# Attention and two feed-forward stages on one core: the operands of the next token tile, the places of the buffers, the leaky function, and full rows in the attention

## The chip, the cores and the metric

One Trainium2 chip, one core. The metric is the device time of one launch in microseconds (us), the median of several runs. TensorE (PE) multiplies, VectorE (DVE), ScalarE (ACT) and GpSimd (POOL) work on elements, SyncE (SP) issues the transfers. SBUF is the working memory, PSUM the eight banks that PE writes.

## What is computed

Three stages, all in float32, each on the result of the one before:

- attention: 4 batches, 8 heads, 576 positions, head size 64; causal, with a decay bias from a running sum of max(s, 0): `softmax(q k^T / 8 + min(bias, 0)) v`
- experts: 2304 tokens of width 512, 8 experts of width 1024; every token goes through every expert: `out += P[:, e] * (max(x @ w1[e], 0) @ w2[e])`, where P comes from 8 rounds of normalising the gate over rows and columns
- last stage: `h = x @ w_in` (width 2048), `g = max(0.01 h, h)`, `out = g @ w_out`

## The kernel before

**Units.** Experts and last stage run over three tiles of 2 x 384 tokens (j = 0, 1, 2). A unit is one tile against 256 columns of the first weight and the 256 rows of the second that go with them: 32 units for each tile in the experts (n = 0 to 95), 8 in the last stage (96 to 119). A tile change is at n = 32, 64, 96, 104 and 112.

**First product.** It is done in seven products of half size (P1 to P7, Strassen's scheme in Winograd's form), on sums and differences of quarters of the token tile (the operands, x = 0 to 6) and of the weight (made in `weights1`). Every operand is held as a high part and a low part (what the high part lacks), and a product is six matmuls of 384 columns: high x high, high x low, low x high, for two halves of the width (`product`, L809 to L811).

**Operands of a tile** (`operands`). Four differences on DVE (L161), for which there are two places, XT[0] and XT[1], each used twice: `b12 - b11`, `b22 - XT[0]`, `b22 - b12`, `b21 - XT[1]`. Seven casts on ACT to the high parts XO (L154), and seven subtractions to the low parts (L156), five on DVE and two on POOL. XO exists once. So the third difference waits for the cast and subtraction of the first, and each operand of the new tile waits until the last product of the old one that reads it is done. All have key n - 0.5 and wait for `("begun", n - 1)`, the first product of the unit before.

**After the products** (`first`). PE adds products up in four banks a, b, c, d; DVE adds what is common (L818). `out` then makes a block of the hidden layer, 384 columns in a high part hh and a low part hl (tile HB). Experts: ACT takes max(., 0) from the bank to hh (L830), DVE subtracts hh from the bank (L831). Last stage, four steps: ACT copies the bank to G (L835), DVE takes max(0.01 x bank, G) to G (L836), ACT casts G to hh (L837), DVE subtracts hh from G (L838).

**Second product** (`second`). Six chunks a unit, c0 to c5, six matmuls of 512 columns each (L877 to L879), in three Y banks in turn, which DVE adds to acc (L896 experts, L902 last stage). They run one unit late, between the products: P1, P6, c0, P5, c1, P7, c2, P2, c3, P4, c4, P3, c5.

**Other work of DVE.** The weights of the last stage come in 64-bit form and are made to float32 in 32 conversions of eight steps (L780 to L787), one in every odd unit from 9 to 71. At the end of each expert tile PE turns the 24 blocks of acc into X (L914).

**Order.** Nothing is scheduled by the chip: `Plan.order` plays all tasks through with estimated times, gives each engine the ready task with the lowest key, and the program is written out in that order. Each engine then works strictly in it. A unit n has keys n to n + 1.

**Attention.** 16 pairs of heads. Per pair: loads (`load_raw`), transposes of q and k in five blocks, the fifth with the 64 rows that are left (`t_pe`, L367), scores (L416 to L422), maximum and exponential, transposes of the result (L469, L471), and the product with v in `pv0` and `pv1`, the last part again with 64 rows (L497).

Of the kernel before, what the change touches and what calls it, by code (L numbers as in the profile page):

```python
# [102 lines left out]
def fused_kernel(ctx: ExitStack, tc: tile.TileContext, q, k, v, s, w_gate, w1, w2, w_in, w_out, out):  # L103
# [18 lines left out]
    wg = const.tile([128, 4, 32], F32, name="wg")  # L122
    P = const.tile([128, NTT, E], F32, name="P")

# [22 lines left out]

    def operands(do, j, key, rd=None):
        t0, t1 = slice(W * j, W * j + W), slice(HALF + W * j, HALF + W * j + W)
        b11, b12, b21, b22 = X[:, 0:2, t0], X[:, 0:2, t1], X[:, 2:4, t0], X[:, 2:4, t1]  # L150
        rd = rd or [("X", j)]

        def split(i, src, res, lo_eng):
            do("act", key + 0.001 * i, pa(768), lambda: nc.scalar.copy(XO[:, i, 0], src), res, [("xh", i)])  # L154
            do(lo_eng, key + 0.001 * i, pd(768) if lo_eng == "dve" else pgg(768),
               lambda: (nc.vector if lo_eng == "dve" else nc.gpsimd).tensor_tensor(out=XO[:, i, 1], in0=src, in1=XO.bitcast(F32)[:, i, 0], op=ALU.subtract),  # L156
               res + [("xh", i)], [("xl", i)])

        def comb(eng, i, dst, x, y, res, out):
            do(eng, key + 0.001 * i - 0.002, pd(768) if eng == "dve" else pgg(768),  # L160
               lambda: (nc.vector if eng == "dve" else nc.gpsimd).tensor_tensor(out=dst, in0=x, in1=y, op=ALU.subtract), res, [out])  # L161

        comb("dve", 0, XT[0], b12, b11, rd, "xt0")
        comb("dve", 0, XT[1], b22, XT[0], rd + ["xt0"], "xt1")
        split(0, b11, rd, "dve")
        split(1, XT[1], ["xt1"], "dve")
        split(2, XT[0], ["xt0"], "pool")
        comb("dve", 3, XT[0], b22, b12, rd, "xt0")
        split(3, XT[0], ["xt0"], "dve")
        split(4, b21, rd, "pool")  # L170
        comb("dve", 5, XT[1], b21, XT[1], rd + ["xt1"], "xt1")
        split(5, XT[1], ["xt1"], "dve")
        split(6, b22, rd, "dve")
# [55 lines left out]
    with ExitStack() as actx:  # L229
# [24 lines left out]
        PC = [ac.tile([128, 4, 2, 320], F32, name=f"PC{i}") for i in range(PB)]  # L254
        PD = [ac.tile([64, 2, 64], F32, name=f"PD{i}") for i in range(PB)]
        EB = ac.tile([128, NE, 512], F32, name="EB")
# [104 lines left out]
        def t_pe(p, which, raw, first=False):  # L361
# [3 lines left out]
            for t in range(5):  # L365
                w = 128 if t < 4 else TAIL
                nc.tensor.transpose(tp[0:n, 128 * t:128 * t + w], raw[0:w, t, 0:n // 64, :].rearrange("p h d -> p (h d)"), ident[0:w, 0:w])  # L367

# [104 lines left out]
        def p_copy(n, part, eng):  # L473
# [3 lines left out]
            if part == 1:  # L477
                dst, src = PD[p % PB], t[0:TAIL, 0, :].rearrange("p (h q) -> p h q", h=2)
            elif i == 8:
# [24 lines left out]
        def pv1(p, part):  # L504
# [38 lines left out]
        for p in range(2):  # L543
            add(("L", "v", p), "sp", -5 + 4 * p, 950, lambda p=p: load_raw(RV[p], v, p), [("qd", 0, 1), ("kd", 0, 1)], DMA)
        add(("c0",), "dve", -40, 370, relu_s, [("s",)])
# [267 lines left out]
    def first(n):  # L813
# [11 lines left out]
        def out(block, bank, key):  # L825
# [3 lines left out]
            if kind == "moe":  # L829
# [3 lines left out]
                return  # L833
            g = G[block]
# [87 lines left out]
    for n, (kind, j, u) in enumerate(seq):  # L922
# [42 lines left out]
```

## Time and profile before

| | |
|---|---|
| runs, us | 2203.02, 2204.18, 2206.31; median 2204.18 |
| profiled execution | 2205.11 us, span on the core 2203.3 us |
| busy share | PE 97%, DVE 75%, POOL 64%, ACT 41% |
| mean granted clock of PE | 0.988 |
| attention | about 0 to 230 us |
| experts, units 0 to 95 | about 230 to 1790 us |
| last stage, units 96 to 119 | about 1790 to 2203 us |

Starts of the sixth product (bank b, L809 FB), which mark a unit: 731.4 (n = 31), 751.2 (32), 777.9 (33), 794.1 (34), 1251.8 (63), 1773.1 (95), 1905.5 (103), 2040.5 (111). Away from tile changes they lie 15.76 us apart.

In the rows below, `[2.55 <-DVE HB L831]` means that the engine stood idle for 2.55 us before this instruction, and that DVE's work of line 831 on tile HB released it. In groups, `xN | busy, mean` is the number of instructions, their us in all and the mean in ns.

### The profile page before, as it was taken

Reading aid. Unit: us, or ns where it says so; the run is one execution under the profiler, and the core shown is the slowest. Engines: PE = TensorE matmul, PEld = TensorE weight load, DVE = VectorE, ACT = ScalarE, POOL = GpSimd, SP = SyncE. Lnnn points to the kernel's source line nnn. Section 1 sums busy time; section 2 is a strip of 40 time slices with the busy share of each in tenths; the row PEclk is TensorE's granted clock in tenths of the full one; section 3 lists DMA queues with packets and bytes.
Section 4 is the critical chain, followed back from the end, with each engine's and each line's share of the span. In section 5 each row is a group of like instructions: output and inputs, shape, how many; then the busy total and the mean of one; then the engine's idle time right before and its main releaser. Section 6 shows DMA issues by size and latency. Waiting matters only on the chain.

```text
span 2203.3 us, 30513 instructions
## 1 busy us (share of the span) xinstructions
PE 2139.7 (97%) x10919; PEld 1879.8 (85%) x10919; DVE 1661.7 (75%) x2800; ACT 900.1 (41%) x1746; POOL 1406.5 (64%) x1207
## 2 busy tenths in 40 slices
PE   7998999999999899999999989999999999999899
PEld 6776689999999798999999878899999988889798
DVE  5888486887788878788778878765656577978877
ACT  5887423232323342333333343333333344444542
POOL 6777656666666666666666656656565676766662
PEclk9999999999999999999999989999999999999999
DMA  6553212222332222232323222222222222122221
GB/s 146 133 135 84 87 58 68 96 87 90 96 96 82 76 87 90 96 96 81 97 96 96 72 86 72 81 65 68 67 68 66 69 65 64 51 97 66 86 68 48
DMA packets 177057, 183.78 MB, mean 83 GB/s; under 512 B 69866, under 2 KB 131306, under 8 KB 176906
## 3 DMA queue, kind: packets, MB, share of 16 engines
q1 hardware_dynamic: 176906, 181.84, 27.7%
q8 instruction: 86, 1.41, 0.3%
q14 instruction: 65, 0.53, 0.1%
HBM read 158.67 MB, written 13.42 MB: 78 GB/s over the span
## 4 chain that ended last, share of the span: by engine, by line
PE 87%; DVE 9%; issue 2%; ACT 1%; POOL 1%; SPq 0%; DMA 0%; POOLq 0%; ACTq 0%; DVEq 0%
PE Y L877 14%; PE Y L879 14%; PE Y L878 14%; PE FC L809 4%; PE FD L809 4%; PE FA L809 4%; PE FC L810 4%; PE FD L811 4%; PE FC L811 4%; PE FD L810 4%; PE FA L811 4%; PE FA L810 4%; PE FB L811 2%; PE FB L809 2%; PE FB L810 2%
## 5 line engine op out<-in xcount | busy, mean ns | idle before, releaser
L189 POOL TENSOR_TENSOR WQ<-RB,WQ 128x512 fp32r<-128x512 f32 x360 | 558.1, 1556 | 671.7 <-ACT WQ L209 357.3
L877 PE MATMUL Y<-WQ,HB 128*128 128x512 f32 x1440 | 569.3, 395 | 4.3 <-DVE acc L896 4.3
L879 PE MATMUL Y<-WQ,HB 128*128 128x512 f32 x1440 | 569.0, 395 | 2.5 <-DVE HB L831 2.5
L878 PE MATMUL Y<-WQ,HB 128*128 128x512 f32 x1440 | 566.4, 393 | 0.0
L896 DVE SCALAR_TENSOR_TENSOR acc<-Y,P,acc 128x512 f32<-128x512 f32 x504 | 375.6, 745 | 205.2 <-PE Y L879 205.0
L189 POOL TENSOR_TENSOR RB<-RB 128x256 f32<-128x256 f32 x480 | 375.7, 803 | 10.2 <-DMA RB<-in_moe_w_dram 0.7
L879 PEld LDWEIGHTS Y<-WQ,HB 128*128 128x128 f32 x1440 | 271.5, 189 | 65.4 <-DVE HB L831 2.9
L189 POOL TENSOR_TENSOR WQ<-RAW,WQ 128x1024 fp32r<-128x1024 f32 x120 | 301.1, 2509 | 18.9 <-ACT WQ L226 18.9
L830 ACT ACTIVATE HB<-FB 128x384 fp32r<-128x384 f32 x96 | 47.2, 492 | 633.0 <-DVE FB L818 632.9
L877 PEld LDWEIGHTS Y<-WQ,HB 128*128 128x128 f32 x1440 | 271.8, 189 | 37.7 <-DVE acc L896 5.0
L878 PEld LDWEIGHTS Y<-WQ,HB 128*128 128x128 f32 x1440 | 273.4, 190 | 32.2
L809 PE MATMUL FA<-XO,WQ 128*128 128x384 f32 x480 | 167.4, 349 | 8.1 <-DVE HB L831 6.4
L809 PE MATMUL FD<-XO,WQ 128*128 128x384 f32 x480 | 166.3, 347 | 9.0 <-DVE G L836 7.3
L809 PE MATMUL FC<-XO,WQ 128*128 128x384 f32 x480 | 165.1, 344 | 7.2 <-DVE G L836 5.1
L811 PE MATMUL FA<-XO,WQ 128*128 128x384 f32 x480 | 164.4, 343 | 0.0
L810 PE MATMUL FA<-XO,WQ 128*128 128x384 f32 x480 | 163.6, 341 | 0.0
L811 PE MATMUL FD<-XO,WQ 128*128 128x384 f32 x480 | 163.4, 341 | 0.0
L811 PE MATMUL FC<-XO,WQ 128*128 128x384 f32 x480 | 163.1, 340 | 0.0
L810 PE MATMUL FD<-XO,WQ 128*128 128x384 f32 x480 | 163.0, 340 | 0.0
L810 PE MATMUL FC<-XO,WQ 128*128 128x384 f32 x480 | 162.7, 339 | 0.0
L211 ACT CAST WQ<-RB 128x1024 fp32r<-128x1024 f32 x120 | 125.6, 1046 | 90.2 <-PE FC L810 85.8
L226 ACT CAST WQ<-RAW 128x1024 fp32r<-128x1024 f32 x120 | 126.1, 1051 | 15.9 <-PE Y L879 10.3
(165 smaller groups left out, 3976.5 us busy)
## 6 DMA issues: line engine op xcount, KB each, us to landing
RB<-in_moe_w_dram SPq DMA_DIRECT2D x96, 512.0 KB
RAW<-in_moe_w_dram SPq DMA_DIRECT2D x96, 512.0 KB, 3.7
RB<-win SPq DMA_DIRECT2D x24, 512.0 KB
RAW<-wout SPq DMA_DIRECT2D x24, 512.0 KB, 3.8
bits<-in_moe_w_in_dram SPq DMA_DIRECT2D x16, 512.0 KB, 5.7
bits<-in_moe_w_out_dram SPq DMA_DIRECT2D x16, 512.0 KB
WQ<-WQ SPq DMA_DIRECT2D x48, 144.0 KB, 2.3
RB<-in_k_dram SPq DMA_DIRECT2D x31, 160.0 KB, 2.9
```

The costliest lines, as they stand in the source:

```text
L189: return lambda: nc.gpsimd.tensor_tensor(out=out, in0=x, in1=y, op=op)
L211: do("act", key + 0.04, pa(1024), lambda: nc.scalar.copy(wa[0][:, 0:4], SW), ss, [("wh0", s)])
L226: do("act", key + 0.5, pa(1024), lambda: nc.scalar.copy(wb[0], RAW2), ["raw2"], [("vh", s)])
L809: nc.tensor.matmul(t, lhsT=hi, rhs=xh, start=new, stop=False, skip_group_check=on)
L810: nc.tensor.matmul(t, lhsT=hi, rhs=xl, start=False, stop=False, skip_group_check=on)
L811: nc.tensor.matmul(t, lhsT=lo, rhs=xh, start=False, stop=(k == 1), skip_group_check=on)
L830: do("act", key, pa(W), lambda: nc.scalar.activation(out=hh, in_=src, func=ACTF.Relu), [bank], [("hh", slot)])
L877: nc.tensor.matmul(y, lhsT=hh, rhs=wb[0][:, f], start=(f == 0), stop=False)
L878: nc.tensor.matmul(y, lhsT=hh, rhs=wb[1][:, f], start=False, stop=False)
L879: nc.tensor.matmul(y, lhsT=hl, rhs=wb[0][:, f], start=False, stop=(f == 1))
L896: do("dve", k2, pd(512), lambda a=a, y=y, p=p: nc.vector.scalar_tensor_tensor(out=a, in0=y, scalar=p, in1=a, op0=ALU.mult, op1=ALU.add), [ ...
```

## The change

- The four differences of the next tile have a place each (XT[0], XT[1] and two halves of GG, the former G) and keys n - 2.6 to n - 1.7; they wait for `("begun", n - 3)`. The casts and low parts have keys 0.6 of a unit before the product that reads them. For tile 0 of the experts, made within the attention, all stays but small shifts of keys.
- Conversions leave out units 31, 33, 63 and 65 and go on to unit 79.
- P moves from the first pool to the later one; with two unused tiles (320 and 832 bytes) X, WQ, XO, XT and RB lie 256 bytes lower, RAW2 and G 320 bytes and HB, acc and the tiles after them 1152 bytes higher than before.
- Last stage: ACT applies Prelu in the bank, ACT copies the bank to hh, DVE subtracts hh from the bank.
- Attention: all five transposes take 128 rows; the last part of the product with v takes 128 rows, of which 64 are zeros (set once), so v is loaded in two transfers a head instead of one.

```diff
-    P = const.tile([128, NTT, E], F32, name="P")
+    const.tile([128, 80], F32, name="room")
...
-    def operands(do, j, key, rd=None):
+    def operands(do, j, early, late, rd, room=None):
...
-            do("act", key + 0.001 * i, pa(768), lambda: nc.scalar.copy(XO[:, i, 0], src), res, [("xh", i)])
+            do("act", late[i], pa(768), lambda: nc.scalar.copy(XO[:, i, 0], src), res, [("xh", i)])
...
+        D = XT + (room or XT)
+        names = ["xt0", "xt1"] + (["xt2", "xt3"] if room else ["xt0", "xt1"])
+        parts = [lambda: comb(0, D[0], b12, b11, rd, names[0]),
+                 lambda: comb(1, D[1], b22, D[0], rd + [names[0]], names[1])]
+        more = [lambda: comb(2, D[2], b22, b12, rd, names[2]),
+                lambda: comb(3, D[3], b21, D[1], rd + [names[1]], names[3])]
+        for f in parts + (more if room else []):
+            f()
...
+        def load_v(p):
...
+                nc.sync.dma_start(out=RV[p % 2][:, 0:4, hh, :], in_=flat[r0:r0 + 512].rearrange("(t p) d -> p t d", p=128))
+                nc.sync.dma_start(out=RV[p % 2][0:TAIL, 4, hh, :], in_=flat[r0 + 512:r0 + S])
...
+            for i in range(2):
+                nc.gpsimd.memset(RV[i][TAIL:128, 4, :, :], 0.0)
+                nc.gpsimd.memset(PD[i][TAIL:128, :, :], 0.0)
...
-                nc.tensor.transpose(tp[0:n, 128 * t:128 * t + w], raw[0:w, t, 0:n // 64, :].rearrange("p h d -> p (h d)"), ident[0:w, 0:w])
+                nc.tensor.transpose(tp[0:n, 128 * t:128 * t + 128], raw[:, t, 0:n // 64, :].rearrange("p h d -> p (h d)"), ident)
...
-                                 (768, 64, TAIL, 4, lambda h: d_[:, h, :], False, True)])
+                                 (768, 64, 128, 4, lambda h: d_[:, h, :], False, True)])
...
+    P = wp.tile([128, NTT, E], F32, name="P")
...
-    G = [wp.tile([128, W], F32, name=f"G{i}") for i in range(4)]
+    GG = wp.tile([128, 4, W], F32, name="GG")
+    G = [GG[:, i] for i in range(4)]
+    wp.tile([128, 208], F32, name="room2")
...
-            do("act", key, pa(W), lambda: nc.scalar.copy(g, src), [bank], [("g", block)])
-            do("dve", key, pd(W), lambda: v.scalar_tensor_tensor(out=g, in0=src, scalar=0.01, in1=g, op0=ALU.mult, op1=ALU.max), [bank], [("g", block)])
-            do("act", key + 0.01, pa(W), lambda: nc.scalar.copy(hh, g), [("g", block)], [("hh", slot)])
-            do("dve", key + 0.02, pd(W), lambda: v.tensor_tensor(out=hl, in0=g, in1=hh.bitcast(F32), op=ALU.subtract), [("g", block), ("hh", slot)], [("hl", slot)])
+            do("act", key, pa(W), lambda: nc.scalar.activation(out=src, in_=src, func=ACTF.Prelu, alpha=0.01), [], [bank])
+            do("act", key, pa(W), lambda: nc.scalar.copy(hh, src), [bank], [("hh", slot)])
+            do("dve", key, pd(W), lambda: v.tensor_tensor(out=hl, in0=src, in1=hh.bitcast(F32), op=ALU.subtract), [bank, ("hh", slot)], [("hl", slot)])
...
-            operands(do, j, n - 0.5, [("X", j), ("begun", n - 1)])
+            operands(do, j, [n - 2.6 + 0.3 * i for i in range(4)], [n - 0.6 + at[x] for x in ("P1", "P6", "P5", "P7", "P2", "P4", "P3")],
+                     [("X", j), ("begun", n - 3)], [GG[:, 0:2], GG[:, 2:4]])
...
-        if 9 <= n < 9 + 64 and n % 2:
+        if 9 <= n < 80 and n % 2 and n not in (31, 33, 63, 65):
```

## Rows read from the trace of the kernel before

**Rows 1.** Busy by stretch: five engines (instructions), granted clock, DMA share, GB/s.
```profile
605.30:636.80 31.50, 31.50 (x157) 28.39 (x156) 25.33 (x39) 10.35 (x19) 20.27 (x17) 1.00 0.30 92
699.80:715.60 15.80, 15.80 (x80) 14.25 (x79) 15.70 (x23) 4.79 (x9) 10.54 (x9) 1.00 0.20 58
715.60:731.40 15.80, 15.80 (x80) 14.24 (x80) 9.74 (x17) 5.67 (x11) 9.82 (x9) 1.00 0.39 126
731.40:794.10 62.70, 53.67 (x259) 47.02 (x258) 54.06 (x65) 27.39 (x46) 37.17 (x27) 0.92 0.25 76
1251.80:1315.40 63.60, 56.07 (x260) 48.70 (x260) 54.20 (x65) 27.48 (x46) 37.27 (x27) 0.87 0.23 75
1773.10:1826.70 53.60, 50.49 (x259) 44.57 (x258) 41.96 (x56) 29.65 (x53) 37.78 (x27) 1.00 0.19 59
1858.20:1889.80 31.60, 31.60 (x159) 28.48 (x158) 26.80 (x39) 14.03 (x27) 21.14 (x17) 1.00 0.22 68
1905.50:1946.00 40.50, 33.70 (x158) 29.55 (x158) 37.15 (x49) 18.43 (x34) 24.91 (x18) 0.96 0.19 64
2040.50:2081.80 41.30, 35.29 (x158) 30.88 (x158) 36.94 (x49) 19.82 (x35) 27.51 (x19) 0.92 0.24 77
```

**Rows 2.** Order of time: PE in one pair of the attention, around five transposes.
```profile
88.15 0.27 PE L471 MATMUL tr<-ident,EAB 128*64 128x128 f32 x1
88.26 0.80 PE L367 MATMUL qk<-ident,RB 128*128 128x128 f32 x5
88.99 0.40 PE L421 MATMUL sc<-WQ 128*128 128x288 f32 x1
```

**Rows 3.** Order of time at unit 32: PE instructions that waited (start, us).
```profile
747.00 0.51 PE L877 MATMUL Y<-WQ,HB 128*128 128x512 f32 x1 [2.17 <-DVE acc L896]
...
751.23 0.41 PE L809 MATMUL FB<-XO,WQ 128*128 128x384 f32 x1 [2.55 <-DVE HB L831]
...
756.20 0.69 PE L809 MATMUL FA<-XO,WQ 128*128 128x384 f32 x1 [3.68 <-DVE HB L831]
```

**Rows 4.** Groups by line on DVE from 250 us on, shapes apart.
```profile
L161 DVE TENSOR_TENSOR XT<-X,XT 128x768 f32<-128x768 f32 x10 | 16.4, 1644 | 0.0
L161 DVE TENSOR_TENSOR XT<-X 128x768 f32<-128x768 f32 x10 | 16.3, 1627 | 0.0
L156 DVE TENSOR_TENSOR XO<-X,XO 128x768 fp32r<-128x768 f32 x10 | 20.4, 2040 | 0.0
L156 DVE TENSOR_TENSOR XO<-XT,XO 128x768 fp32r<-128x768 f32 x15 | 20.2, 1356 | 0.0
L836 DVE SCALAR_TENSOR_TENSOR G<-FA,G 128x384 f32<-128x384 f32 x24 | 13.3, 554 | 7.6 <-ACT G L835 7.6
L838 DVE TENSOR_TENSOR HB<-G,HB 128x384 fp32r<-128x384 f32 x96 | 106.1, 1108 | 8.9 <-ACT HB L837 7.3
L831 DVE SCALAR_TENSOR_TENSOR HB<-FA,HB 128x384 fp32r<-128x384 f32 x95 | 52.5, 552 | 21.5 <-ACT HB L830 21.4
```

**Rows 5.** Order of time: starts of P1, P6 and the chunk behind them.
```profile
730.29 0.34 PE L809 MATMUL FA<-XO,WQ 128*128 128x384 f32 x1
...
731.36 0.33 PE L809 MATMUL FB<-XO,WQ 128*128 128x384 f32 x1
...
732.40 0.39 PE L877 MATMUL Y<-WQ,HB 128*128 128x512 f32 x1
```

**Rows 6.** Order of time on ACT: the only load of a table.
```profile
0.73 1.28 ACT L331 ACT_TABLE_LOAD   x1 [0.73 <-PEq L949]
```

**Rows 7.** Chain of work that ended last, one pair of the attention (start, us).
```profile
64.89 1.09 DVE sm L456
...
70.85 0.45 PE sc L416
...
77.04 1.08 DVE sm L456
```

**Rows 8.** Order of time on SP: loads of v for the first pairs.
```profile
16.63 2.23 SPq L296 DMA_DIRECT2D RV<-in_v_dram  x4
```

More of the change, by code (lines that the diff above doesn't have):

```diff
@@ L145, in fused_kernel @@
     pgg = lambda n: 92.0 + n * 2.3
-    def operands(do, j, key, rd=None):
+    def operands(do, j, early, late, rd, room=None):
         t0, t1 = slice(W * j, W * j + W), slice(HALF + W * j, HALF + W * j + W)
         b11, b12, b21, b22 = X[:, 0:2, t0], X[:, 0:2, t1], X[:, 2:4, t0], X[:, 2:4, t1]
-        rd = rd or [("X", j)]
         def split(i, src, res, lo_eng):
-            do("act", key + 0.001 * i, pa(768), lambda: nc.scalar.copy(XO[:, i, 0], src), res, [("xh", i)])
-            do(lo_eng, key + 0.001 * i, pd(768) if lo_eng == "dve" else pgg(768),
+            do("act", late[i], pa(768), lambda: nc.scalar.copy(XO[:, i, 0], src), res, [("xh", i)])
+            do(lo_eng, late[i], pd(768) if lo_eng == "dve" else pgg(768),
@@ L156, in split @@
                lambda: (nc.vector if lo_eng == "dve" else nc.gpsimd).tensor_tensor(out=XO[:, i, 1], in0=src, in1=XO.bitcast(F32)[:, i, 0], op=ALU.subtract),
                res + [("xh", i)], [("xl", i)])
[L159 to L163, printed above, removed]
@@ L164, in operands, with comb @@
-        comb("dve", 0, XT[1], b22, XT[0], rd + ["xt0"], "xt1")
-        split(0, b11, rd, "dve")
[L166 to L169, printed above, removed]
+        def comb(i, dst, x, y, res, out):
+            do("dve", early[i], pd(768), lambda: nc.vector.tensor_tensor(out=dst, in0=x, in1=y, op=ALU.subtract), res, [out])
+        D = XT + (room or XT)
+        names = ["xt0", "xt1"] + (["xt2", "xt3"] if room else ["xt0", "xt1"])
@@ new lines, in operands @@
+        parts = [lambda: comb(0, D[0], b12, b11, rd, names[0]),
[4 more added lines that the diff above has]
+            f()
+        split(0, b11, rd, "dve")
+        split(1, D[1], [names[1]], "dve")
+        split(2, D[0], [names[0]], "pool")
+        if not room:
+            more[0]()
@@ L170, in operands @@
+        split(3, D[2], [names[2]], "dve")
         split(4, b21, rd, "pool")
-        comb("dve", 5, XT[1], b21, XT[1], rd + ["xt1"], "xt1")
-        split(5, XT[1], ["xt1"], "dve")
+        if not room:
+            more[1]()
+        split(5, D[3], [names[3]], "dve")
         split(6, b22, rd, "dve")
@@ L254, in fused_kernel @@
         PC = [ac.tile([128, 4, 2, 320], F32, name=f"PC{i}") for i in range(PB)]
-        PD = [ac.tile([64, 2, 64], F32, name=f"PD{i}") for i in range(PB)]
+        PD = [ac.tile([128, 2, 64], F32, name=f"PD{i}") for i in range(PB)]
         EB = ac.tile([128, NE, 512], F32, name="EB")
@@ L287, in side @@
             return {"a": "act", "d": "dve"}[KEYS["cq" if p % 2 else "cp"][i]]
+        def load_v(p):
+            b, hp = divmod(p, HP)
+            flat = v.rearrange("b h n d -> (b h n) d")
+            for hh in range(2):
+                r0 = (b * H + 2 * hp + hh) * S
+                nc.sync.dma_start(out=RV[p % 2][:, 0:4, hh, :], in_=flat[r0:r0 + 512].rearrange("(t p) d -> p t d", p=128))
+                nc.sync.dma_start(out=RV[p % 2][0:TAIL, 4, hh, :], in_=flat[r0 + 512:r0 + S])
         def load_raw(dst, src, p, heads=(0, 1)):
@@ L365, in t_pe @@
             for t in range(5):
-                w = 128 if t < 4 else TAIL
-                nc.tensor.transpose(tp[0:n, 128 * t:128 * t + w], raw[0:w, t, 0:n // 64, :].rearrange("p h d -> p (h d)"), ident[0:w, 0:w])
+                nc.tensor.transpose(tp[0:n, 128 * t:128 * t + 128], raw[:, t, 0:n // 64, :].rearrange("p h d -> p (h d)"), ident)
         def q_hi(p, h):
@@ L477, in p_copy @@
             if part == 1:
-                dst, src = PD[p % PB], t[0:TAIL, 0, :].rearrange("p (h q) -> p h q", h=2)
+                dst, src = PD[p % PB][0:TAIL], t[0:TAIL, 0, :].rearrange("p (h q) -> p h q", h=2)
             elif i == 8:
@@ L543, in fused_kernel @@
         for p in range(2):
-            add(("L", "v", p), "sp", -5 + 4 * p, 950, lambda p=p: load_raw(RV[p], v, p), [("qd", 0, 1), ("kd", 0, 1)], DMA)
+            add(("L", "v", p), "sp", -5 + 4 * p, 950, lambda p=p: load_v(p), [("setc",), ("qd", 0, 1), ("kd", 0, 1)], DMA)
         add(("c0",), "dve", -40, 370, relu_s, [("s",)])
@@ L566, in fused_kernel @@
                     add(("L", w, p), "sp", b9 - KEY["L"], 950, lambda raw=raw, src=src, p=p: load_raw(raw[p % 2], src, p), [("T", w, p - 2)] + [("L", x, 1) for x in "qkv"], DMA)
-                add(("L", "v", p), "sp", b9 - KEY["L"] + 3, 950, lambda p=p: load_raw(RV[p % 2], v, p), [("pv1", p - 2, 1), ("pv0", p - 2, 0)], DMA)
+                add(("L", "v", p), "sp", b9 - KEY["L"] + 3, 950, lambda p=p: load_v(p), [("pv1", p - 2, 1), ("pv0", p - 2, 0)], DMA)
             if p:
@@ L643, in fused_kernel @@
             plan.writer["X", 0, p] = d["xc", p]
-        operands(plan.do, 0, 9 * NPAIR - 6, [("X", 0, p) for p in (0, 1, 2, 3, 8, 9, 10, 11)])
+        operands(plan.do, 0, [9 * NPAIR - 6 + 0.001 * i for i in (-2, -1, 3, 5)], [9 * NPAIR - 6 + 0.001 * i for i in range(7)],
+                 [("X", 0, p) for p in (0, 1, 2, 3, 8, 9, 10, 11)])
         plan.do("sp", -6, 100, lambda: nc.sync.dma_start(out=wgraw, in_=w_gate.rearrange("(c p) e -> p c e", p=128)), [], ["wgraw"], DMA)
@@ L833, in out @@
                 return
-            g = G[block]
-            do("act", key, pa(W), lambda: nc.scalar.copy(g, src), [bank], [("g", block)])
-            do("dve", key, pd(W), lambda: v.scalar_tensor_tensor(out=g, in0=src, scalar=0.01, in1=g, op0=ALU.mult, op1=ALU.max), [bank], [("g", block)])
-            do("act", key + 0.01, pa(W), lambda: nc.scalar.copy(hh, g), [("g", block)], [("hh", slot)])
-            do("dve", key + 0.02, pd(W), lambda: v.tensor_tensor(out=hl, in0=g, in1=hh.bitcast(F32), op=ALU.subtract), [("g", block), ("hh", slot)], [("hl", slot)])
+            do("act", key, pa(W), lambda: nc.scalar.activation(out=src, in_=src, func=ACTF.Prelu, alpha=0.01), [], [bank])
+            do("act", key, pa(W), lambda: nc.scalar.copy(hh, src), [bank], [("hh", slot)])
+            do("dve", key, pd(W), lambda: v.tensor_tensor(out=hl, in0=src, in1=hh.bitcast(F32), op=ALU.subtract), [bank, ("hh", slot)], [("hl", slot)])
         pe("P1")
```

## Prediction

> **What bounds the kernel now.** I read first the busy time by stretch, then the groups of instructions on VectorE (DVE), then single stretches in order of time. In a plain stretch of the experts TensorE (PE) is busy for all of 31.50 us, which is two units (78 matmuls each), so a unit takes 15.75 us; the same holds in the last stage, 31.60 us for two units and a rest [rows 1]. There nothing but the matmuls counts. The time that can be had lies where a token tile ends and the next begins, five times (units 32, 64, 96, 104, 112). The stretch of units 31 to 33 lasts 62.70 us instead of 47.25; 24 transposes of the finished tile belong in it, at 0.11 us each [rows 2] 2.6 us, so 12.8 us are lost. In the same way 63.60 gives 13.7 and 53.60 gives 3.7 (three units and the transposes each), 40.50 gives 9.0 and 41.30 gives 9.8 (two units) [rows 1]. Together 49 us. PE's waits there end with DVE: 2.17 us for an addition to acc, 2.55 and 3.68 us for the low part of a hidden block [rows 3]. Of that loss a part is the clock: it is granted at 0.92, 0.87, 1.00, 0.96 and 0.92 in the five stretches and at 1.00 beside them [rows 1], and as its other level is half, 0.08 of 62.70 us is 5 us of matmul time given away after the waits. If the waits go, that goes with them.
>
> Why DVE is late: a unit with a conversion takes 15.70 us of DVE in 15.80, one without 9.74, so a conversion is 6.0 us [rows 1]. A tile change adds four differences, two of 1.627 and two of 1.644 us, 6.5 us, and five low parts, two of 2.040 and three of 1.356, 8.1 us [rows 4]. Units 31 and 32 of before thus ask for 9.7 x 2 + 6.0 + 6.5 + 8.1 = 40 us of DVE in 31.5.
>
> **Part 1: differences early, in four places.** They keep their 6.5 us, but may run from unit n-3 on, as they no longer wait for a place that a low part still reads. The conversions of units 31, 33, 63 and 65 go to 73 to 79, where DVE has 6.0 us free in every unit without one [rows 1]. What is left in units n-1 and n: 9.7 x 2 + 8.1 = 27.6 of 31.5 us for units 32, 64 and 96; removed are 12.5 us at the first two and 6.5 at the third, against losses of 12.8, 13.7 and 3.7. Splits now carry keys beside the product that reads them, 0.6 of a unit (9.4 us) ahead. Where the differences land nothing is free at once: units 29 and 30 hold 15.70 + 9.74 + 6.5 = 31.9 us in 31.5. DVE leaves unit 29 up to 3 us behind and is level again in unit 31. Behind a late difference in DVE's queue stand the additions to acc; PE has three Y banks and a chunk every 2.4 us, some 4.8 us of cover. I take 1.5 us of waits left at units 32 and 64 (bounds: nothing, and half the present loss, 6.5) and 0.3 at each of the other three.
>
> **Part 2: leaky function in the bank.** Per block, DVE loses the maximum (0.554 us), and its subtraction reads a bank instead of G: 0.552 us, as the same operation in the experts takes, instead of 1.108 [rows 4]. Four blocks a unit: 4 x (0.554 + 0.556) = 4.4 us off 13.4 (half of 26.80 [rows 1]). ScalarE (ACT) still has two operations of a block each. The bank is held for one more ACT copy, about 0.5 us by the nearest of its kind, and c is wanted again 4.9 us after its last product (a chunk, two products, a chunk; a product is 1.06 us [rows 5], so a chunk (15.75 - 7 x 1.06) / 6 = 1.4), which covers it. At units 104 and 112 DVE has (13.4 - 4.4) x 2 + 8.1 = 26.1 of 31.5 us left to do, where it had 41.4: the 9.0 and 9.8 go but for the 0.3 each. Everywhere else in the last stage PE does not wait, so 4.4 us a unit buys nothing there.
>
> The Trainium skill ("ScalarE: Activation LUTs", section "Table sets: the hidden batching unit") says that cheap functions are in every set, and that a function of another set costs a load. The trace shows one load of 1.28 us for Copy, Relu and Exp together [rows 6]; Prelu is in no row.
>
> Sum of parts 1 and 2: 49 - (2 x 1.5 + 3 x 0.3) = 45 us.
>
> **Part 3: full rows in the attention.** The five transposes of q or k take 0.73 us from 88.26 to 88.99, where five full ones at 0.11 (88.15 to 88.26) would take 0.55 [rows 2]: 0.18 us each, twice a pair, and about as much for the tail of the product with v. That would be 0.54 x 16 = 9 us, were PE the bound all the way. The chain of waits says otherwise: in a pair of 12.15 us (64.89 to 77.04) it is on DVE and ACT up to 70.85 and on PE from there [rows 7]. Only what is saved after 70.85 counts, one group of transposes a pair; the other and the tail of v lie beside the DVE stretch, and PE waits there that much longer. 0.18 x 13 pairs in this rhythm: 2.3 us. Bounds 0 and 9.
>
> The Trainium skill ("TensorE: Matmul & The Clock Gate", section "LDWEIGHTS (loading the stationary operand)") says that columns count and rows don't. By that, 64 more columns in each of 32 groups would cost 0.05 x 32, about 2 us, and save nothing. The row speaks against it: the 64-row step and the one ahead of it are the slow ones.
>
> SP issues four loads of v more before the first pairs, at 2.23 / 4 = 0.56 us each: 2.2 us [rows 8], and the bias of pair 1 is queued behind them. I take 1 us of it on the path (0 to 2.2). Later pairs have two loads more per 12 us; fourteen at 0.56 us are 8 us of SP, and v is wanted a pair later. The four memsets stand on POOL ahead of these loads and are in this term.
>
> **Part 4: places.** All buffers from X on move down by 256 bytes, HB and acc up by 1152; the matmuls stay the same. No row shows a matmul at another place. The nearest: two blocks of the same six matmuls, 1.07 and 1.04 us (730.29, 731.36, 732.40) [rows 5], 178 and 173 ns a matmul, so 5 ns either way on 9360 matmuls, -47 to +47 us as far bounds. I take 0: the slow and the fast block read slices of the same tiles, a whole number of 512 bytes apart, and differ by where they stand in the order.
>
> **Forecast.** 45 + 2.3 - 1 = 46 to 47 us. The profiled execution took 2205.1 us (span 2203.3), 0.04% over the median of 2204.2, which is less than two runs differ. 2204.2 - 47 = 2157 us.
>
> **Rivals.**
> *The wait moves ahead.* Units 29 and 30 are over-full by the sum above, and 61 and 62 as well. If the additions to acc fall behind there, PE waits and the clock falls before the tile change instead of at it. For: 31.9 of 31.5 us. Against: DVE stood at 15.70 of 15.80 in unit 29 without one wait of PE. Units 32 and 64 would then give back half, 13 us, and the ends of the last stage keep 2 each: 2157 + 13 - 3 + 6 = 2173 us.
> *Table loads.* If Prelu's table lacks Copy, each block of the last stage brings two loads: 8 x 1.28 = 10.3 us a unit on top of 7.0 (half of 14.03), 17.3 in 15.75, so 1.5 x 24 = 37 us: 2194 us. For it: no row has Prelu. Against: one load served three functions. The Trainium skill ("ScalarE: Activation LUTs", section "What ACT_TABLE_LOAD costs") gives a switch 2.66 us with its drain, by which this rival would be estimated at 8 x 2.66 + 7.0 - 15.75 = 12.5 us a unit, 300 us in all.
> *Places cost.* If the moved addresses put every matmul 5 to 7 ns up, 47 to 65 us come on top: 2204 to 2222 us, slower than before. It decides from 47 us / 9360 = 5.0 ns a matmul; two ns would take 19 us. The same mechanism with the other sign gives 2110. Against: both slots of the weights, 22 KB apart, run at one pace in every plain stretch.
> *It does not do what it says.* The planner may set the differences late all the same, since it counts 0.9 us for what takes 1.6. Then only the conversions and the leaky function help: 12 of 26 us at units 32 and 64, 9 of 19 in the last stage, so 2204 - 22 = 2182 us.
>
> **How the numbers follow.** Forecast with its own range 2150 to 2166: 0.68. The wait moves ahead: 0.14. Not as it says: 0.06. Table loads: 0.05. Places slower: 0.05, faster: 0.02. For 8 in 10 I go from 2146 (all 49 us and the 9 of the attention) to 2176 (past the first rival). A measurement here tells 0.2%, 4.4 us, from no change. Faster: 0.68 + 0.14 + 0.06 + 0.04 + 0.02, 0.94 less 0.01 for what I haven't seen, 0.93. Within 0.2%: 0.03. Slower: 0.04.
>
> **What would show it.** Right: the five stretches last 50 to 52 us (units 31, 63, 95 on) and 32 (103, 111), the clock at 1.00 in all; the four differences stand in units 29 and 30 with 1.6 us each; the subtraction of the last stage takes 0.55 us; one or two table loads; a group of five transposes takes 0.55 us while a pair shrinks by about 0.2 us; a plain unit still takes 15.75. Wrong: PE waiting for acc in units 29 to 31, a plain unit at another length than 15.75, or ACT over 15 us a unit in the last stage.

## The result, and the profile after

The changed kernel takes 2143.99 us (four runs, 2143.90 to 2144.54), the kernel before, run beside it, 2203.60: a ratio of 0.9729 [0.9712, 0.9746]. The forecast was 2157 with a range of 2146 to 2176, so the time lies 13 us under the forecast and 2 us under the low end of the range. The page of the changed kernel, busy time and share of each engine:

```profile
span 2142.0 us, 30363 instructions
...
PE 2101.8 (98%) x10919; PEld 1850.8 (86%) x10919; DVE 1567.1 (73%) x2704; ACT 897.3 (42%) x1746; POOL 1406.6 (66%) x1211
```

Busy time by stretch, as in [rows 1]: units 29 and 30, the five tile changes and, in the last row, two plain units of the changed kernel (a plain unit is one away from the tile changes).

```profile
693.20:724.50 31.30, 31.01 (x155) 27.46 (x154) 29.72 (x42) 9.82 (x19) 22.11 (x17) 1.00 0.29 93
725.10:775.50 50.40, 49.90 (x260) 44.57 (x260) 31.83 (x45) 27.45 (x46) 36.09 (x27) 1.00 0.21 63
1230.70:1281.10 50.40, 49.94 (x260) 44.61 (x259) 31.74 (x45) 27.36 (x46) 36.08 (x27) 1.00 0.21 63
1735.40:1785.80 50.40, 49.94 (x260) 44.60 (x260) 31.24 (x44) 29.86 (x53) 36.02 (x27) 1.00 0.20 63
1864.20:1896.20 32.00, 31.54 (x157) 28.03 (x157) 25.96 (x36) 18.84 (x34) 24.50 (x19) 1.00 0.27 89
1990.30:2021.50 31.20, 31.20 (x157) 28.06 (x156) 25.67 (x35) 19.24 (x34) 26.30 (x19) 1.00 0.33 107
618.20:649.50 31.30, 31.30 (x158) 28.13 (x157) 24.91 (x39) 10.50 (x18) 21.18 (x17) 1.00 0.29 94
```

The five tile changes went from 62.70, 63.60, 53.60, 40.50 and 41.30 us [rows 1] to 50.40 three times, 32.00 and 31.20, all at a granted clock of 1.00: the forecast's part. But two plain units are also shorter, and PE is busy for all of them in both kernels. Read from the starts of the sixth product in both traces (the loss of a unit is what it takes over the plain unit of its kernel, the transposes left in; counted are units 29 to 35, 61 to 67, 93 to 97, 101 to 105 and 109 to 113):

| part of the time | forecast, us | the two traces, us |
|---|---|---|
| five tile changes, with the units beside them | -45 | 56.8 to 13.2: -43.6 |
| pace of a plain unit, 15.76 to 15.64, 119 units | 0 | -14.3 |
| start of the experts, 230.1 to 226.5 | -1.3 | -3.6 |
| the other units | 0 | +0.5 |
| sum, up to the last unit | -46 | -61.0 |

The two profiled executions differ by 61.3 us in their spans, the medians of the runs by 59.6.

The pace sits in one place. Take the time from the first start of a block of six matmuls to the first start of the next block, median over all units: a product that follows a chunk took 1064 ns and takes 1044; P6, which follows a product, 1040 in both; a chunk 1389 in both. Six products at 20 ns are the 0.12 us of a unit. (The expectations below count matmul by matmul and are 1 or 2 ns off these: 1065, 1043, 1038.) The six matmuls of one such product of the changed kernel, and the next chunk's first:

```profile
606.67 0.33 PE L833 MATMUL FA<-XO,WQ 128*128 128x384 f32 x1
606.84 0.34 PE L834 MATMUL FA<-XO,WQ 128*128 128x384 f32 x1
607.02 0.33 PE L835 MATMUL FA<-XO,WQ 128*128 128x384 f32 x1
607.20 0.33 PE L833 MATMUL FA<-XO,WQ 128*128 128x384 f32 x1
607.37 0.33 PE L834 MATMUL FA<-XO,WQ 128*128 128x384 f32 x1
607.54 0.33 PE L835 MATMUL FA<-XO,WQ 128*128 128x384 f32 x1
607.72 0.39 PE L899 MATMUL Y<-WQ,HB 128*128 128x512 f32 x1
```

### The profile page after: what moved, and what is told of

Same layout as the page of the kernel before. It is cut to its first block, busy times and chain, and to the rows that moved or that the text cites. A ratio compares the mean times of both kernels' runs of the same rounds, so it can differ in the third digit from the quotient of the medians.

```text
span 2142.0 us, 30363 instructions
## 1 busy us (share of the span) xinstructions
PE 2101.8 (98%) x10919; PEld 1850.8 (86%) x10919; DVE 1567.1 (73%) x2704; ACT 897.3 (42%) x1746; POOL 1406.6 (66%) x1211
## 4 chain that ended last, share of the span: by engine, by line
PE 86%; DVE 8%; issue 2%; DMA 2%; ACT 1%; POOL 1%; SPq 0%; POOLq 0%; DVEq 0%; ACTq 0%
PE Y L901 15%; PE Y L900 14%; PE Y L899 14%; PE FC L833 4%; PE FD L834 4%; PE FC L834 4%; PE FD L833 4%; PE FD L835 4%; PE FC L835 4%; PE FA L834 4%; PE FA L833 3%; PE FA L835 3%; PE FB L833 2%; PE FB L835 2%; PE FB L834 2%
## 5 line engine op out<-in xcount | busy, mean ns | idle before, releaser
L197 POOL TENSOR_TENSOR WQ<-RB,WQ 128x512 fp32r<-128x512 f32 x360 | 550.2, 1536 | 628.4 <-ACT WQ L217 358.4
L197 POOL TENSOR_TENSOR RB<-RB 128x256 f32<-128x256 f32 x480 | 386.1, 826 | 11.0 <-DMA RB<-win 1.3
L219 ACT CAST WQ<-RB 128x1024 fp32r<-128x1024 f32 x120 | 126.3, 1053 | 93.1 <-PE FC L834 84.0
L833 PE MATMUL FC<-XO,WQ 128*128 128x384 f32 x480 | 162.0, 338 | 3.0 <-DVE HB L855 2.5
L834 PE MATMUL FD<-XO,WQ 128*128 128x384 f32 x480 | 162.1, 338 | 0.0
L833 PE MATMUL FA<-XO,WQ 128*128 128x384 f32 x480 | 161.6, 337 | 0.3 <-ACT Up L863 0.3
L834 PE MATMUL FA<-XO,WQ 128*128 128x384 f32 x480 | 161.8, 337 | 0.0
L834 PE MATMUL FC<-XO,WQ 128*128 128x384 f32 x480 | 161.8, 337 | 0.0
L833 PE MATMUL FD<-XO,WQ 128*128 128x384 f32 x480 | 161.7, 337 | 0.0
L835 PE MATMUL FD<-XO,WQ 128*128 128x384 f32 x480 | 160.8, 335 | 0.0
L835 PE MATMUL FC<-XO,WQ 128*128 128x384 f32 x480 | 160.5, 334 | 0.0
L835 PE MATMUL FA<-XO,WQ 128*128 128x384 f32 x480 | 160.4, 334 | 0.0
L924 DVE TENSOR_TENSOR acc<-Y,acc 128x512 f32<-128x512 f32 x126 | 86.6, 688 | 68.6 <-PE Y L901 68.4
```

What stands on the lines that cost most here:

```text
L197: return lambda: nc.gpsimd.tensor_tensor(out=out, in0=x, in1=y, op=op)
L219: do("act", key + 0.04, pa(1024), lambda: nc.scalar.copy(wa[0][:, 0:4], SW), ss, [("wh0", s)])
L833: nc.tensor.matmul(t, lhsT=hi, rhs=xh, start=new, stop=False, skip_group_check=on)
L834: nc.tensor.matmul(t, lhsT=hi, rhs=xl, start=False, stop=False, skip_group_check=on)
L835: nc.tensor.matmul(t, lhsT=lo, rhs=xh, start=False, stop=(k == 1), skip_group_check=on)
L924: do("dve", k2, pd(512), lambda a=a, y=y: nc.vector.tensor_tensor(out=a, in0=y, in1=a, op=ALU.add), [yr], [ar])
```

## The experiments

### Which place sets the pace

Four runs on one chip. The first is the kernel before with the placement alone, the second the changed kernel without it:

```diff
# a1_place_alone, from the kernel before (a2_no_place: the same three lines undone in the changed kernel)
-    P = const.tile([128, NTT, E], F32, name="P")
+    const.tile([128, 80], F32, name="room")
...
+    P = wp.tile([128, NTT, E], F32, name="P")
...
+    wp.tile([128, 208], F32, name="room2")
```

> The kernel before with the placement alone: P moved and the two unused tiles added, so that X, WQ, XO and all that follows stand at the changed kernel's addresses; no other edit. Theory (the places set the pace of the first products): each product behind a chunk takes 1.043 us instead of 1.065, a plain unit 15.64 us instead of 15.76, and the kernel gets about 14 us faster, 2190 us; tile changes and attention stay as before. Rival (the pace comes from the work that the other parts moved on the other engines): the plain unit stays at 15.76 and the time at 2204.

> The changed kernel with the placement undone: P back in the first pool, both unused tiles gone, all buffers at the addresses of before; the other three parts stay. Theory (places): the plain unit is 15.76 us again and the kernel takes 2158, 14 us more than the changed kernel, and that is what the forecast of 2157 described. Rival (pace from the other parts): 15.64 and 2144.

Measured: the placement alone 2188.91, ratio 0.9936 [0.9921, 0.9950], a plain unit 15.64; without it 2156.74, ratio 0.9788 [0.9773, 0.9803], a plain unit 15.76. The placement is worth 15 us on the kernel before and 13 on the changed one, and what was left without it is the forecast's 2157. That it is so to the microsecond is luck in part: 1.3 us of the forecast are the attention's, of which c1 below finds nothing.

The other two tell HB from X, WQ and XO:

```diff
# a3_hb_old, from the changed kernel
-    wp.tile([128, 208], F32, name="room2")
+    wp.tile([128, 432], F32, name="room2")
# a4_x_old, from the changed kernel
-    const.tile([128, 80], F32, name="room")
+    const.tile([128, 144], F32, name="room")
...
-    wp.tile([128, 208], F32, name="room2")
+    wp.tile([128, 144], F32, name="room2")
```

> The changed kernel, with the second unused tile larger, so that HB, acc and what follows stand at their old phase (HB 192 bytes past a multiple of 256 instead of 64) while X, WQ and XO stay at the new addresses. If HB's place (read by the chunks) sets the pace: products behind a chunk 1.065 us again, the unit 15.76, 2158 us. If the place of X, WQ and XO sets it: 15.64 and 2144.

> The changed kernel, with the first unused tile 256 bytes larger and the second smaller by as much and some, so that X, WQ, XO, XT and RB stand where they stood before and HB and acc where the change put them. If the place of WQ and XO sets the pace: products behind a chunk 1.065 us again, the unit 15.76, 2158 us. If HB's place sets it: 15.64 and 2144.

Measured: HB at its old phase 2157.07, ratio 0.9788 [0.9773, 0.9802]; X, WQ and XO at their old places 2144.07, 0.9733 [0.9717, 0.9749]. One product and the next chunk with HB at its old phase, in order of time, to be held against the seven rows of the changed kernel:

```profile
606.48 0.34 PE L833 MATMUL FD<-XO,WQ 128*128 128x384 f32 x1
606.65 0.34 PE L834 MATMUL FD<-XO,WQ 128*128 128x384 f32 x1
606.83 0.34 PE L835 MATMUL FD<-XO,WQ 128*128 128x384 f32 x1
607.00 0.35 PE L833 MATMUL FD<-XO,WQ 128*128 128x384 f32 x1
607.19 0.34 PE L834 MATMUL FD<-XO,WQ 128*128 128x384 f32 x1
607.37 0.34 PE L835 MATMUL FD<-XO,WQ 128*128 128x384 f32 x1
607.54 0.40 PE L899 MATMUL Y<-WQ,HB 128*128 128x512 f32 x1
```

From the first start to the chunk's 1.06 us here, 1.05 there; the fourth matmul alone goes from 185 to 173 ns in the medians. These six matmuls do not read HB. The chunks on both sides of them do: HB is what they hold as weights.

### Phases against each other

The phase of a tile is what its address has left over when divided by 256 bytes.

```diff
# a5_acc_old, from the changed kernel (ahead of acc)
+    wp.tile([128, 224], F32, name="room3")
# a6_hb_64, a7_hb_128: room2 with 224 and 240 columns instead of 208
# a8_all_128: room with 112 columns instead of 80
# d1_xo_128: ahead of XO, and room2 with 176 columns (d2_xo_hb_128: room2 as it was)
+    xpool.tile([128, 32], F32, name="room1")
```

> The changed kernel with 896 unused bytes between HB and acc: HB stands where the change put it, acc and the buffers behind it stand at their old phase (192 past a multiple of 256). Theory (HB's place alone, since PE reads HB as the weights of the chunks and never reads acc): 15.64 us a unit, 2144. Rival (acc's place, which VectorE reads and writes at every chunk): 15.76 and 2157.

> The changed kernel with HB and acc 64 bytes higher (HB 128 past a multiple of 256, 128 past one of 512). No row says which places are slow; 64 past a multiple of 256 (and of 512) is fast, 192 (448 past a multiple of 512) is slow. If a place is slow when a row of 512 bytes of HB starts off a multiple of 128: fast or faster here, 2144 or less, by as much as 22 ns a product again at most. If only the place of after is fast: 15.76 us a unit, 2157.

> The changed kernel with HB and acc 128 bytes higher (HB 192 past a multiple of 256, and of 512). If the phase within 256 bytes decides: slow like before, 15.76 us a unit, 2157. If the phase within 512 or 2048 decides (before: 448 of 512, 1472 of 2048): it can be fast, 15.64 and 2144.

> The changed kernel with everything from X on 128 bytes higher: X, WQ, XO and HB all 192 past a multiple of 256. If HB's own phase within 256 bytes decides (192 was slow twice, with WQ and XO at 64): 15.76 us a unit, 2157. If the phase of HB against WQ and XO decides (equal is fast): 15.64 and 2144.

> The changed kernel with 128 unused bytes between WQ and XO, taken out again ahead of HB: XO stands 192 past a multiple of 256, WQ and HB 64. The runs so far say that HB and the group of WQ and XO must have one phase within 256 bytes. If it is HB against WQ (both are read in one matmul of a chunk): 15.64 us a unit, 2144. If it is HB or WQ against XO (the products read WQ and XO, and they are what slows): 15.76 or more, 2157 or more; P6, which follows a product, then tells WQ against XO (slow too) from HB against XO (1038 ns as before).

> As the run with XO alone 128 bytes up, but HB goes up with it: XO and HB 192 past a multiple of 256, WQ 64. If HB against XO decides: 15.64 us a unit, 2144. If HB against WQ, or WQ against XO: 15.76 or more, 2157 or more.

Measured; the addresses are those of the program, as bytes past a multiple of 256, the three times in ns are the medians of a block's first start to the next block's. One P6, six other products and six chunks add up to the unit:

| kernel | WQ, XO, HB | P6 | product behind a chunk | chunk | plain unit, us | time, us |
|---|---|---|---|---|---|---|
| before | 64, 64, 192 | 1040 | 1064 | 1389 | 15.76 | 2203.6 |
| changed | 64, 64, 64 | 1040 | 1044 | 1389 | 15.64 | 2143.99 |
| a3, a7 | 64, 64, 192 | 1040 | 1064 | 1389 | 15.76 | 2157.07, 2157.34 |
| a6 | 64, 64, 128 | 1043 | 1060 | 1400 | 15.80 | 2162.43 |
| a8 | 192, 192, 192 | 1040 | 1044 | 1389 | 15.64 | 2143.96 |
| d1 | 64, 192, 64 | 1053 | 1052 | 1375 | 15.61 | 2142.61 |
| d2 | 64, 192, 192 | 1049 | 1052 | 1392 | 15.71 | 2153.10 |

a5 (acc at its old phase, HB not) has 15.64 and 2145.94: acc, which PE reads only for the transposes of a finished tile, plays no part. a8 against a7 says that it is not HB's own phase: 192 is slow beside 64 and fast beside 192. What counts is how the tiles stand to each other within 256 bytes; a4 moved X, WQ and XO by a whole 256 against HB and changed nothing.

d1 and d2 say which pair matters most. HB at 64 instead of 192 is worth 0.12 us a unit with XO at 64 (15.76 to 15.64) and about 0.1 with XO at 192 (15.71 to 15.61); XO at 192 instead of 64 takes off another 0.03 or 0.05. HB against XO decides nothing by itself: equal phases give 15.64 and 15.71, unequal ones 15.76 and 15.61. So most of the effect goes with HB against WQ. Neither expectation had how XO's part comes about: moving XO slows P6 (which reads WQ and XO only) by 13 ns and the other products by 8, and speeds the chunks up by 14, though no chunk reads XO. It would fit that each pair of successive reads has a price of its own and a unit is their sum, but no run shows that, and a law from which the table could be worked out is left open. With XO, d1 and d2 move the buffers behind it too (XT, RB and those up to room2); PE reads none of them in a plain unit, but no run moves XO without them.

The Trainium skill ("SBUF — State Buffer", section "Who interferes with whom") says that PE has two independent read ports, one for what it streams and one for the weights, and that it never waits on anyone. Taken as a rule on pace, that would give every row of the table one unit length. The rows disagree: 15.61 to 15.80 us. What it is in the chip that takes the time, no run here shows.

### What made the tile changes short

```diff
# b1_leaky_alone: the kernel before with the Prelu lines of the change as its only edit
# b2_diff_late, from the changed kernel
-            operands(do, j, [n - 2.6 + 0.3 * i for i in range(4)], ...
-                     [("X", j), ("begun", n - 3)], [GG[:, 0:2], GG[:, 2:4]])
+            operands(do, j, [n - 0.5 + 0.001 * i for i in range(4)], ...
+                     [("X", j), ("begun", n - 1)], [GG[:, 0:2], GG[:, 2:4]])
# b3_conv_old, from the changed kernel
-        if 9 <= n < 80 and n % 2 and n not in (31, 33, 63, 65):
+        if 9 <= n < 9 + 64 and n % 2:
```

> The kernel before with the leaky function in the bank as its only edit (places and operands as before). By the forecast the ends of units 103 and 111 lose 9.0 and 9.8 us, and with the differences still late and late places some of it stays: VectorE has 26 of 31.5 us to do in the two units, so between half and all of 18.8 us goes: 2185 to 2194 us. Rival (the differences' two places are what is waited for there, not VectorE's load): under 4 us gained, 2200 or more.

> The changed kernel with the four differences late again (keys n - 0.5, after the first product of the unit before) but in their own places; casts, low parts, conversions and everything else as changed. Theory (VectorE's load in the two units of a tile change decides): 27.6 + 6.5 = 34.1 of 31.5 us at units 32, 64 and 96 and 26.1 + 6.5 = 32.6 at 104 and 112, so 2.6 us too much three times and 1.1 twice, 10 us, and about as much again where TensorE then starts at the lower clock: 2154 to 2164 us, with waits of TensorE for low parts of HB or XO. Rival (the early keys buy nothing, the conversions and the places of their own did it all): 2144 to 2148.

> The changed kernel with the conversions back in units 31, 33, 63 and 65 (and none in 73 to 79). By the forecast's sum VectorE then has 27.6 + 6.0 = 33.6 us to do in the 31.5 of units 31 and 32, and of 63 and 64: 2.1 us too much twice, and about as much again at the lower clock: 2148 to 2153. Rival (the early differences alone made the room, since unit 33's conversion lies behind the change): 2144 to 2146.

Measured: b1 2190.37, ratio 0.9937 [0.9922, 0.9952]; in its trace the two changes in the last stage lose 2.9 and 2.1 us instead of 8.9 and 9.8, the other three what they lost before. b2 2165.26, ratio 0.9837 [0.9823, 0.9852]; its five changes lose 33.0 us where the changed kernel's lose 13.2. b3 2159.29, ratio 0.9799 [0.9784, 0.9813]; units 29 to 35 and 61 to 67 lose 10.3 and 9.9 instead of 4.1 and 4.3. Both theories held; the tops of their ranges were 1 us (b2) and 6 us (b3) short of the time. In each 3 us of the profiled execution are units 3 and 4 (last section), which the edits don't touch; without them b2 lies within its range and b3 3 us above. PE's only wait of b3 about unit 32, and the busy time of that stretch (units 31 to 33):

```profile
749.40 0.69 PE L833 MATMUL FA<-XO,WQ 128*128 128x384 f32 x1 [3.44 <-ACT Up L863]
```

```profile
728.80:785.20 56.40, 52.94 (x259) 46.73 (x259) 49.69 (x61) 26.99 (x46) 37.11 (x27) 0.94 0.26 84
```

DVE has 49.69 us to do there where the changed kernel has 31.83. The 16 instructions more are two conversions, so each adds 9 us at this place, where the forecast had 6.0. The clock falls to 0.94: the wait is paid twice, as the forecast had it.

### Attention

```diff
# c1_rows_old: the changed kernel with t_pe, the last product of pv1 and the loads of v as before
# c2_no_add, from the changed kernel; e1_rows_old_no_add: both
-            nc.vector.tensor_scalar(out=sm, in0=sm, scalar1=EPS, scalar2=None, op0=ALU.add)
```

> The changed kernel with the attention's 64-row steps back (transposes, tail of the product with v, loads of v in one transfer a head). Theory (the transposes are beside the loop of a pair, which runs over VectorE, ScalarE and GpSimd): pairs stay 12.16 us apart, and what is lost is the 3 to 4 us that the two traces differ by at single pairs outside the rhythm (the first at half clock, pairs 7 and 14): 2147 to 2148. The forecast's reading (0.18 us a pair for 13 pairs, less 1 us of loads): 2145, with pairs 0.18 us longer. Rival (nothing; the attention's 3.6 us came with the places): 2144 with the first unit starting at 225.

> The changed kernel without the addition of 1e-9 to the sums of the exponentials (VectorE, 128 x 3, before the reciprocal; each sum holds a 1, to which 1e-9 adds nothing in float32). In the trace this addition takes 1.39 and 0.90 us in a pair instead of 0.17 whenever GpSimd runs its subtraction for k beside it, and ends with it. Theory (it is in the loop of a pair): up to 1.9 us of VectorE a pair is freed, of which TensorE, busy for 11.58 of 12.16 us, lets at most 0.6 become time: pairs 11.6 to 12.0, 2 to 7 us in all, 2137 to 2142. Rival (the reciprocal behind it is held up in the same way, or another wait ends as late): 12.16 and 2144.

> The changed kernel without the addition of 1e-9 (as that run, 2134, pairs 11.09 us apart with TensorE busy for all of it) and with the attention's 64-row steps back. Theory (a matmul step counts only where TensorE is the bound of the loop, which it now is): three groups a pair at 0.18 us, 0.54 us for 11 pairs and more for the long ones, so pairs 11.6 us apart and 6 to 8 us lost: 2140 to 2142. Rival (the 64-row steps cost no more than the full ones, and the trace's 0.73 us is only how their ends are modelled): 11.09 and 2134.

Measured: c1, which has no zeros to set either, 2146.86 (2143.46 to 2147.44), ratio 0.9748 [0.9732, 0.9765]. The experts start at 226.6 us, with full rows at 226.5, and pairs are 12.17 us apart against 12.16. The 2.9 us of its median are not in the attention: units 3 and 4 took 20.9 and 19.6 us instead of 19.3 and 18.0. Nor are the 3.6 us by which the two first traces differ the change's: b1, whose attention is the one of before, starts the experts at 226.2. Its second pair, from the first product with v to the next pair's, took 17.3 us and not 20.0, which is most of the difference; why is open.

c2 2134.41, ratio 0.9695 [0.9680, 0.9709]. GpSimd and DVE in one pair of the changed kernel:

```profile
63.01 1.42 POOL L426 TENSOR_TENSOR WQ<-KF,WQ 64x576 fp32r<-64x576 f32 x1
...
63.07 1.39 DVE L476 TENSOR_SCALAR sm<-sm 128x3 f32<-128x3 f32 x1
...
64.49 0.18 DVE L477 RECIPROCAL sm<-sm 128x3 f32<-128x3 f32 x1
...
66.46 1.41 POOL L426 TENSOR_TENSOR WQ<-KF,WQ 64x576 fp32r<-64x576 f32 x1
...
66.99 0.90 DVE L476 TENSOR_SCALAR sm<-sm 128x3 f32<-128x3 f32 x1 [0.34 <-ACT EAB L472]
...
67.93 0.18 DVE L477 RECIPROCAL sm<-sm 128x3 f32<-128x3 f32 x1
```

An operation on three columns takes 1.39 and 0.90 us and ends each time with GpSimd's. Such rows look busy, and no wait is shown. The reciprocal in the run without the addition takes 0.17 to 0.18 us and is not held up, though two of the three start while GpSimd is in such a subtraction (the same pair):

```profile
60.98 1.42 POOL L426 TENSOR_TENSOR WQ<-KF,WQ 64x576 fp32r<-64x576 f32 x1
...
61.58 0.17 DVE L476 RECIPROCAL sm<-sm 128x3 f32<-128x3 f32 x1
...
64.10 1.41 POOL L426 TENSOR_TENSOR WQ<-KF,WQ 64x576 fp32r<-64x576 f32 x1
...
64.48 0.18 DVE L476 RECIPROCAL sm<-sm 128x3 f32<-128x3 f32 x1 [0.34 <-ACT EAB L472]
...
68.93 0.18 DVE L476 RECIPROCAL sm<-sm 128x3 f32<-128x3 f32 x1 [0.17 <-ACT EB L472]
```

Busy time of one pair, the changed kernel and then the one without the addition:

```profile
59.99:72.15 12.16, 11.58 (x88) 8.94 (x88) 10.18 (x34) 9.95 (x30) 9.00 (x13) 1.00 0.58 131
```

```profile
58.53:69.62 11.09, 11.09 (x88) 8.93 (x87) 7.99 (x31) 9.95 (x30) 9.03 (x14) 1.00 0.64 146
```

The pair goes from 12.16 to 11.09 us, PE is busy for all of it, and the experts start 12.5 us earlier, 3.1 of which units 3 and 4 give back. The expectation allowed 0.6 us a pair, PE's idle time; it was 1.07, as PE's busy time for the same 88 matmuls fell too, from 11.58 to 11.09: a busy share of 95% was no bound on what a wait in the loop was worth. The Trainium skill ("SBUF — State Buffer", section "Who interferes with whom") says that a tensor_scalar on DVE may take both of its ports, one pair of which it shares with GpSimd, and then blocks for the whole of GpSimd's instruction. The rows of L426 and L476 agree.

e1 2140.72, ratio 0.9709 [0.9694, 0.9723]: pairs of 11.76 us, 0.67 more than with full rows, and the experts 6.2 us later. The same edit that bought nothing at 12.16 us a pair is worth 6 us once PE is the bound.

### A version that beats both

```diff
# d3_best, from c2_no_add
-        if 9 <= n < 80 and n % 2 and n not in (31, 33, 63, 65):
+        if 9 <= n < 84 and n % 2 and n not in (29, 31, 33, 61, 63, 65):
# e2_best_xo: d3_best with room1 and room2 of d1_xo_128
```

> The changed kernel without the addition of 1e-9, and with the conversions of units 29 and 61 moved to 81 and 83 as well. Theory (the 0.6 and 0.9 us that TensorE waits in units 30 and 62 come from the early differences on top of those conversions): both waits go, 1.5 us less than without the addition alone, 2133. Rival (they come from the differences' own place in the order): 2134 to 2135, units 30 and 62 as long as before.

> The best version so far (2133) with 128 unused bytes between WQ and XO, as in the run with XO alone moved (15.61 us a unit, chunks 1376 ns instead of 1389, products 1051 instead of 1043). If the pace depends on the places alone: 0.02 to 0.03 us less in each of some 110 units, 2 to 3 us, 2130 to 2131. Rival (that run's 1.4 us were the spread of executions): 2133.

Measured: d3 2133.18, ratio 0.9679 [0.9662, 0.9695]; units 30 and 62 have their plain length, so the conversion beside the early differences made those waits. Against c2 the times alone don't tell 1.2 us apart; the unit lengths do. e2 2129.31, ratio 0.9659 [0.9643, 0.9675], chunks of 1375 ns and products of 1052 again: the pace goes with the arrangement. Of its 4 us against d3, 3.2 are the pace (0.027 us in 119 units); the rest lies within the spread of units 3 and 4. By the medians it is 14.7 us faster than the changed kernel and 76 faster than the kernel before.

## Why the prediction was wrong

**The failed step is Part 4**, "I take 0: the slow and the fast block read slices of the same tiles, a whole number of 512 bytes apart, and differ by where they stand in the order". The term is -14.3 us in the traces, -13 and -15 by a2 and a1. The row it rested on [rows 5] held the answer: P1 follows a chunk and took 1.07, P6 follows a product and took 1.04. That is the order, as the step said, but what the order brings in is HB, a third tile that the chunks on either side of the product read (a3, a7 and a8), and the change moved HB 1408 bytes against WQ. The step asked whether the block's own operands moved against each other (they don't) and not whether its neighbours' did.

**The range was cut against its own rule.** Part 4 named bounds of -47 and +47 us, and the rival with the other sign 2110; the low end, 2146, held the other terms' best case alone. The rival was priced for every matmul. Slowed are 36 of the 78 of a unit, by 3.3 ns on average.

**The tile changes, Parts 1 and 2, came out as worked out**: 45 forecast, 43.6 in the traces, with b1, b2 and b3 for the parts. The waits that remain are in part a unit ahead of the change, as the first rival had it, at a tenth of its price. Units 30 and 62 of the changed kernel take 0.6 and 0.9 us more than a plain one; PE's waits in them:

```profile
714.21 0.44 PE L833 MATMUL FC<-XO,WQ 128*128 128x384 f32 x1 [0.29 <-DVE HB L855]
...
1215.80 0.44 PE L833 MATMUL FA<-XO,WQ 128*128 128x384 f32 x1 [0.34 <-ACT Up L863]
```

DVE was put at 31.9 us in units 29 and 30 and has 29.72 of 31.30. Most of what it has less is the differences, put at 1.6 us each:

```profile
698.71 0.94 DVE L161 TENSOR_TENSOR XT<-X 128x768 f32<-128x768 f32 x1
...
705.91 0.94 DVE L161 TENSOR_TENSOR XT<-X,XT 128x768 f32<-128x768 f32 x1
...
712.11 1.57 DVE L161 TENSOR_TENSOR GG<-X 128x768 f32<-128x768 f32 x1
...
715.20 1.29 DVE L161 TENSOR_TENSOR GG<-X,XT 128x768 f32<-128x768 f32 x1
```

The subtraction of the last stage was put at 0.552 us, and no load of a table beyond the one of before was counted:

```profile
L860 DVE TENSOR_TENSOR HB<-FA,HB 128x384 fp32r<-128x384 f32 x24 | 13.4, 557 | 13.7 <-ACT HB L859 13.7
```

```profile
L351 ACT ACT_TABLE_LOAD x1 | 1.3, 1283 | 0.7 <-PEq L972 0.7
```

One load in the whole run: the rival of the table loads is out. So is "it does not do what it says": the four differences start in units 29 and 30, and b2 shows what late ones would have cost, 20 us by the unit lengths.

**Part 3, the attention, had the wrong mechanism and a small price.** It read the chain of one pair [rows 7] as a DVE stretch and a PE stretch and counted what PE saves in the second, 2.3 us. c1 measures nothing beyond the spread. The loop of a pair runs through DVE's held-up addition, and what PE saves beside a loop that others set is idle time in either stretch. That PE stood on the chain from 70.85 did not make its steps the limit; 11.58 of 12.16 us busy said that it waited somewhere in every pair. The 1 us for the loads of v is not to be seen either. The steps themselves did get shorter: the five transposes, 0.73 us before [rows 2], take 0.46, and e1 prices the three groups of a pair at 0.67 us where Part 3 had 0.54.

```profile
86.54 0.71 PE L387 MATMUL qk<-ident,RB 128*128 128x128 f32 x5
87.00 0.38 PE L441 MATMUL sc<-WQ 128*128 128x288 f32 x1
```

Nor did that row speak against the rule for weight loads, as Part 3 says: in the kernel before, the load for a 64-row step has 128 columns like the others and takes 136 ns beside 141. The 64 more columns are of what streams past the weights.

```profile
L367 PEld LDWEIGHTS qk<-ident,RB 128*128 128x128 f32 x89 | 10.8, 141 | 2.7
...
L367 PEld LDWEIGHTS qk<-ident,RB 64*128 64x128 f32 x23 | 3.1, 136 | 3.8 <-issue 3.8
```

## What to carry to other kernels

When a change moves buffers, price the matmuls from the blocks that follow each other, not from one block's operands: compare a block behind its like with one behind another kind, and keep the difference as the bound of the range. An operation on a few columns that takes over a microsecond can be a wait in disguise; look for what ends with it on the engine next to it. A saving on an engine counts only where that engine is the bound of the loop; the same edit was worth 0 and 6 us before and after another wait had gone.

## What the runs showed of the hardware

- The pace of full matmul streams depends, in these runs, on how the tiles stand to each other within 256 bytes: 15.61 to 15.80 us for the same 78 matmuls, 1.2%, repeated to 0.01 us (a3 and a7; changed, a4, a5 and a8; d1 and e2). Moving all tiles together by 128 bytes changes nothing (a8).
- A tile that a matmul does not read can slow it, or speed it up, by where it stands: HB the products by 20 ns, XO the chunks by 14 ns in six matmuls.
- Units 3 and 4 together take 37.4 us in some traces and 40.5 in others (39.0 in a7's), for kernels with the same work there: PE's waits for DVE, 2.4 and 1.7 us, are the same, and the granted clock of the stretch is 1.00 in one and 0.92 in the other. Why it falls in one and not in the other is open. The changed kernel and then the one without the addition:

```profile
283.00:321.00 38.00, 33.91 (x169) 29.66 (x168) 35.30 (x79) 10.43 (x18) 19.85 (x17) 1.00 0.18 56
```

```profile
271.00:312.00 41.00, 36.90 (x169) 32.43 (x168) 35.91 (x79) 10.03 (x17) 19.54 (x17) 0.92 0.15 52
```

With the start of the experts, which lies between 224.7 and 227.4 us in traces of one and the same attention, this would account for most of the up to 6 us by which single times of one kernel differ here. It is why small terms were read from unit lengths.
